# A delta-rule attention with a two-layer block behind it: unnormalised key triangles, keys ahead of queries, the first inverses apart, weights in eight pieces, an order table

## The chip, the core and the metric

The kernel runs on one core of a Trainium2 chip. The core has five engines that run side by side, each through its own instructions in order: TensorE (PE in the profile) multiplies matrices and writes to PSUM, VectorE (DVE), ScalarE (ACT) and GpSimd (POOL) work on tiles, and SyncE (SP) issues transfers. An instruction starts when the semaphores that it waits for have been raised; whatever stands behind it on its engine waits with it. The metric is the device time of one execution in microseconds (us). Before the change three runs gave a median of 319.31 us (317.59 to 320.36). The profile is of another execution, with a span of 320.9 us.

## The reference, cut to what matters

```python
k_n = k / (norm(k) + 1e-6)
for t in range(S):                       # S = 768 steps, for 4 batches x 8 heads, D = 48
    y[t]  = g[t] * (q[t] @ state)
    state = state + beta[t] * outer(k_n[t], v[t] - k_n[t] @ state)
x = y of all heads side by side          # 3072 tokens x 384
out = softplus(x @ w_in) @ w_out         # 384 -> 2048 -> 384
```

The recurrence over 768 steps is worked in chunks of 64 steps. In a chunk the update is a triangular system: with the Gram matrix of the chunk's keys, `T = (I + tril(beta K K^T))^-1 beta`, new values `U = T (V - K S)`, output `Q S + tril(Q K^T) U`, new state `S + K^T U`. The next chunk needs the state of the one before, so twelve chunks form a chain. The dense block behind it needs only the finished outputs of the chunks.

## The kernel before

**Tiling.** A tile holds one chunk of 64 steps of two batches on its 128 partitions (`r` picks the upper or lower 64), with a pair of batches `p` and the heads along the free side. A unit `u` is one head of one chunk; 16 units of chunk half `cl` of 0 and 1 make the 32 of a double chunk `cc` (128 steps, six of them). In a unit, rows are in quadrants of 32.

**Stages of a double chunk** (line numbers are those of the profile):

- *front*: the keys are squared on ScalarE (L380), summed on VectorE (L387), a root is taken (ScalarE L404 in the first double chunk, GpSimd `pow` L424 afterwards), 1e-6 is added (L433), inverted (L434), and the keys are scaled by it into float16 `kn` (L446); the queries are cast to `qn` (L467). For each `(cl, p)` TensorE transposes keys and queries together (L489), ScalarE copies all of it into `kqt` (L512), and 32 matmuls form the triangles of keys with keys and keys with queries (L531, L535). ScalarE copies the key part, negated, to `kk` (L553); VectorE masks the query part to `mt` (L572). So a key triangle waits for the norm and for the queries.
- *inverse*: VectorE turns `kk` so that each lane holds one unit (`ln`, L595); two multiplies by beta (L617) and 15 steps of a multiply and an add (L628, L635) invert the 16x16 diagonal blocks in `tt`, on VectorE for `cc` 0 and on GpSimd afterwards. VectorE turns the result back (L661, L683), ScalarE casts it (L671, L691), TensorE builds the 32x32 blocks (L710, L745, L755) and the coupling between them (L796, L799), with ScalarE copies between (L730, L779, L817). Both chunks of a double chunk share one inverse.
- *chain* of a chunk: keys times state (L843), `v` minus it (L886), inverse times it (L899), copy (L925), coupling (L954), copy (L981), state update (L997, L1020), output (L843 again, L1038), times `g` (L1071), transposed (L1088) into `xt` (L1098).
- *dense*: L1122 multiplies `xt` by `w_in` into PSUM `h`, ScalarE takes the softplus (L1143) into `ga`, L1160 multiplies by `w_out` into the one PSUM tile `o`, VectorE copies it out (L1182), SyncE stores it (L1191). The first and the last double chunk do this by single chunks, 256 tokens at a time, the others with 512.

**What sets the order.** Every piece of work is put down with an engine, a cost, its inputs, the buffers that it takes from rings and a priority. `Plan.run` plays the engines forward with these costs and writes the instructions of each engine in the order that comes out: of the ready pieces the one with the lowest priority number. It models transfers and the loading of TensorE's own instructions in blocks of 128 matmuls. On the chip that order is fixed; only the semaphores decide when each begins. Loads go out on SyncE (L299) in a written order: keys 0, queries 0, keys 1, values 0, gates 0, queries 1, values 1, keys 2, gates 1 (each number a double chunk). The two weights are one transfer each on GpSimd (L322, L335), which also turns them from float32 to float16; `w_in` is issued after values 0, `w_out` after queries 1.

Of the kernel before, what the change touches and what calls it, by code (L numbers as in the profile page):

```python
# [16 lines left out]

class Ring:


    def __init__(self, n, make):
        self.n, self.make = n, make
        self.live = 0
        self.freed = [0.0] * n
        self.count = 0


class Buf:
    def __init__(self, ring):
        self.ring = ring  # L30
        self.users = 0
        self.ap = None
        self.done = 0.0


class Item:
    __slots__ = (
        "eng", "cost", "fn", "deps", "bufs", "prio", "end", "tail", "n", "order", "mm", "dma",
# [3 lines left out]
class Plan:  # L42
    BLOCK = 128
    FETCH = 3.5

    def __init__(self):
        self.items = []

    def add(self, eng, cost, fn, deps=(), bufs=(), prio=0, tail=0.1, order=(), mm=0, dma=0):
        it = Item()  # L50
        it.eng, it.cost, it.fn = eng, cost, fn
        it.deps = [d for d in deps if d is not None]
        it.bufs, it.prio, it.tail, it.end = list(bufs), prio, tail, None
        it.n = len(self.items)
        it.order = [d for d in order if d is not None]
        it.mm, it.dma = mm, dma
        for b in it.bufs:
            b.users += 1
        self.items.append(it)
        return it  # L60

    def run(self):

        left = {}
        for it in self.items:
            left.setdefault(it.eng, []).append(it)
        free = {e: 0.0 for e in left}
        pipe = 0.0
        flight = []
        issued, arrive = 0, [0.0, 0.0]  # L70
        while any(left.values()):
            best = None
            for e, lst in left.items():
                cands = []
                for it in lst[:500]:
                    ready = 0.0
                    ok = all(d.end is not None for d in it.order)
                    for d in it.deps:
                        if d.end is None:
                            ok = False  # L80
                            break
                        t = d.end + (d.tail + 0.06 if d.eng != e else 0.0)
                        if t > ready:
                            ready = t
                    if not ok:
                        continue
                    need = {}
                    for b in it.bufs:
                        if b.ap is None:
                            need[b.ring] = need.get(b.ring, 0) + 1  # L90
                    for r, n in need.items():
                        if r.live + n > r.n:
                            ok = False
                            break
                        ready = max(ready, sorted(r.freed)[n - 1])
# [5 lines left out]
                can = [it for r, it in cands if r <= t0 + 1e-9]  # L101
                stall = 0.0
                if e == "PE":

                    def late(it):
                        last = (issued + it.mm - 1) // self.BLOCK
                        return max(0.0, arrive[min(last, len(arrive) - 1)] - t0 - it.cost)
# [3 lines left out]
                it = min(can, key=lambda x: (x.prio, x.n))  # L111
# [6 lines left out]
            for b in it.bufs:  # L118
                if b.ap is None:
                    r = b.ring  # L120
                    r.live += 1
                    r.freed.remove(min(r.freed))
                    b.ap = r.make(r.count)
                    r.count += 1
            it.fn()
            if it.dma:
                if e == "SP" and len(flight) >= 4:
                    t0 = max(t0, flight[-4])
                free[e] = t0 + it.cost
                pipe = max(pipe, free[e] + 0.6) + it.dma  # L130
                it.end = pipe + 1.4
                if e == "SP":
                    flight.append(it.end)
            else:
                it.end = free[e] = t0 + it.cost
            if e == "PE":
                block = issued // self.BLOCK
                issued += it.mm
                end = it.end
# [4 lines left out]
                it.end = free[e] = end  # L144
            for b in it.bufs:
                b.users -= 1
                b.done = max(b.done, it.end + it.tail)
                if b.users == 0:
                    b.ring.live -= 1
                    b.ring.freed.append(b.done)  # L150
        return max(free.values())
# [3 lines left out]
def kernel(  # L155
# [24 lines left out]
    consts = ctx.enter_context(tc.tile_pool(name="consts", bufs=1))  # L180
    pool = ctx.enter_context(tc.tile_pool(name="rings", bufs=1))
    psum = ctx.enter_context(
        tc.tile_pool(name="psum", bufs=1, space=bass.MemoryType.PSUM)
# [4 lines left out]
    def ring(name, n, shape, dt, where=pool):  # L188
        return Ring(n, lambda i: where.tile(shape, dt, tag=name, bufs=n, name=name))

    def fixed(name, n, shape, dt, init):
        tiles = [consts.tile(shape, dt, name=f"{name}{i}") for i in range(n)]
        for t in tiles:
            init(t)
        return Ring(n, lambda i: tiles[i % n])

    half_c = consts.tile([P, 32], F32, name="half_c")
    nc.vector.memset(half_c, 0.5)
    dummy = consts.tile([P, 1], F32, name="dummy")
    nc.scalar.activation(dummy, half_c[:, :1], AF.Sqrt)
    ident32 = consts.tile([P, P], F32, name="ident32")
    make_identity(nc, ident32)
    ident = consts.tile([P, P], F16, name="ident")
    nc.vector.tensor_copy(ident, ident32)
    beta_l = consts.tile([P, NSS, HC], F32, name="beta_l")

# [12 lines left out]
    mask = consts.tile([P, C], F16, name="mask")  # L223
# [11 lines left out]
    w_in = consts.tile([P, 3, FF], F16, name="w_in")  # L235
    w_out = consts.tile([P, NF, DM], F16, name="w_out")

    def pad0(t):
        nc.vector.memset(t[:, :, :, D:], 0.0)

    r_k = ring("kf", 4, [P, 2, H, D], F32)
    r_q = ring("qf", 3, [P, 2, H, D], F32)
# [3 lines left out]
    r_ss = ring("ss", 3, [P, 32], F32)  # L246
    r_kn = fixed("kn", 4, [P, 2, H, 64], F16, pad0)
    r_qn = fixed("qn", 2, [P, 2, H, 64], F16, pad0)

    r_kqt = ring("kqt", 10, [P, 2 * NP, 2 * C], F16)  # L250
    r_mt = ring("mt", 18, [P, NP, C], F16)
    r_kk = ring("kk", 2, [P, 2, U, HC], F16)
    r_ln = ring("ln", 1, [P, HC, HC], F16)
    r_n = ring("nn", 1, [P, 2, 16, 16], F32)

    r_t = fixed("tt", 1, [P, 2, 16, 48], F32, lambda t: nc.gpsimd.memset(t, 0.0))
    r_tmp = ring("tmp", 1, [P, 128], F32)
    r_t32 = ring("t32", 1, [P, HC, U], F32)
    r_tn = ring("tn", 2, [P, U, 16], F16)
    r_xs = ring("xs", 2, [P, U, 16], F16)  # L260
    r_td = ring("td", 2, [P, U, HC], F16)
    r_tn32 = ring("tn32", 1, [P, 16, U], F32)
    r_z = ring("z", 2, [P, U, HC], F16)
# [6 lines left out]
    r_o = ring("osb", 4, [P, DM], F32)  # L270
    p_d = ring("d", 5, [P, 512], F32, psum)
    p_h = ring("h", 2, [P, 512], F32, psum)
    p_o = ring("o", 1, [P, 512], F32, psum)

# [12 lines left out]


# [3 lines left out]
    def load(name, x, r, cc):  # L292
        for cl in range(2):
            b = Buf(r)
            t0 = cc * 128 + cl * C

            def fn(b=b, t0=t0, x=x):
                for b2 in range(2):
                    nc.sync.dma_start(  # L299
                        out=b.ap[64 * b2 : 64 * b2 + 64].rearrange(  # L300
# [925 lines left out]
```

## Time and profile before

| | |
|---|---|
| median of three runs | 319.31 us (317.59 to 320.36) |
| span of the profiled execution | 320.9 us |
| TensorE busy | 242.5 us (76%), 6384 matmuls |
| ScalarE, VectorE, GpSimd busy | 157.4, 134.9, 109.3 us |
| dense matmuls L1122 and L1160 | 77.0 and 73.6 us of TensorE's busy time |
| first L1122, first L1160 | at 74.2 and 84.9 us |
| loads of one chunk of one input | two transfers of 192 KB |
| `w_in`, `w_out`, issue to landing | 11.4 and 15.5 us |

The busy times overlap and are means over stages with different limits. The view of busy time by stretches shows where TensorE works, the lines of one engine in order of time show what its queue stood behind. A matmul's listed duration includes the pipeline; the distance between starts tells what the array can do. "issue" as releaser is time in which an engine waited for nothing that the profile shows.

### The profile page before, as it was taken

How to read it: one execution, taken by the hardware profiler on the slowest of the kernel's cores; microseconds unless marked ns; L12 is line 12 of the kernel's file. 1: busy time of each engine (PE TensorE's matmuls, PEld its weight loads, DVE VectorE, ACT ScalarE, POOL GpSimd, SP SyncE). 2: the span in 40 equal slices, each digit the busy share in tenths (PEclk: the TensorE clock that was granted, in tenths of full speed). 3: DMA queues.
4: the chain of work that ended last, by engine and by line, in shares of the span. 5: the costliest groups of instructions: out<-in, count | busy, mean ns of one | idle time of the engine just before them, and what ended most of it. 6: DMA issues, size and time to landing. Idle time of an engine off the chain costs nothing.

```text
span 320.9 us, 13899 instructions
## 1 busy us (share of the span) xinstructions
PE 242.5 (76%) x6384; PEld 160.9 (50%) x6384; DVE 134.9 (42%) x278; ACT 157.4 (49%) x272; POOL 109.3 (34%) x202
## 2 busy tenths in 40 slices
PE   0361081259769999988973969999799998998993
PEld 0240061247557775535653735566455565565761
DVE  2559635216452548573280548455053621321001
ACT  2381081534565654964463545745566247720630
POOL 8154133892015001889840061860008500000000
PEclk9999999999796999997985589999789999999999
DMA  8999999984980167921249390641100121012122
GB/s 117 165 163 182 181 170 192 158 121 86 154 157 8 29 121 137 167 53 27 53 85 144 61 144 3 102 89 41 29 2 4 30 51 29 4 25 51 25 50 51
DMA packets 106458, 27.73 MB, mean 86 GB/s; under 512 B 100768, under 2 KB 106016, under 8 KB 106400
## 3 DMA queue, kind: packets, MB, share of 16 engines
q1 hardware_dynamic: 103680, 23.60, 47.8%
q0 software_dynamic: 2720, 3.24, 6.0%
q8 instruction: 50, 0.82, 1.1%
q14 instruction: 8, 0.07, 0.1%
HBM read 25.26 MB, written 4.72 MB: 93 GB/s over the span
## 4 chain that ended last, share of the span: by engine, by line
PE 62%; DMA 8%; issue 8%; SPq 8%; ACT 5%; POOL 5%; DVE 4%; ACTq 0%; POOLq 0%
PE o L1160 19%; PE h L1122 19%; SPq L299 8%; DMA kf<-in_k_dram 4%; DMA qf<-in_q_dram 4%; PE d L489 3%; PE d L843 3%; PE d L1038 2%; PE d L954 2%; POOL tt L635 2%; PE d L899 2%; PE d L755 2%; POOL tmp L628 2%; PE d L799 2%; PE d L710 2%
## 5 line engine op out<-in xcount | busy, mean ns | idle before, releaser
L1143 ACT ACTIVATE ga<-h 128x512 f16<-128x512 f32 x96 | 57.0, 598 | 48.1 <-PE h L1122 46.2
L1122 PE MATMUL h<-xt,w_in 128*128 128x512 f16 (+1 forms) x384 | 77.0, 341 | 1.0 <-ACT ga L1143 0.9
L1160 PE MATMUL o<-w_out,ga 128*128 128x384 f16 x384 | 73.6, 333 | 2.8 <-DVE osb L1182 2.6
L1160 PEld LDWEIGHTS <-ga 128*128 128x128 f16 x384 | 36.5, 99 | 27.3 <-issue 5.8
L1122 PEld LDWEIGHTS <-w_in 128*128 128x128 f16 x384 | 35.4, 101 | 22.1 <-issue 3.4
L424 POOL TENSOR_TENSOR ss<-ss,half_c 128x32 f32<-128x32 f32 (+1 forms) x6 | 27.6, 4604 | 45.4 <-DVE ss L387 45.4
L1071 DVE TENSOR_TENSOR yg<-d,gf 128x384 f16<-128x384 f32 x24 | 13.2, 552 | 57.6 <-PE d L1038 49.1
L1182 DVE COPY osb<-o 128x384 f32<-128x384 f32 x24 | 13.3, 553 | 53.4 <-PE o L1160 53.3
L512 ACT COPY kqt<-d 128x1024 f16<-128x1024 f16 x24 | 23.7, 1012 | 23.2 <-PE d L489 23.2
L635 POOL TENSOR_TENSOR tt<-tt,tmp 128x30 f32<-128x30 f32 (+7 forms) x75 | 30.0, 400 | 5.9
L628 POOL TENSOR_TENSOR tmp<-nn,tt 128x30 f32<-128x30 f32 (+7 forms) x75 | 27.8, 370 | 5.9
L617 POOL TENSOR_TENSOR nn<-ln,beta_l 128x256 f32<-128x256 f16 x10 | 6.0, 618 | 54.6 <-DVE ln L595 54.6
L489 PE MATMUL d<-ident,qn 128*128 128x128 f16 x96 | 12.4, 269 | 15.9 <-POOL qn L467 14.7
L572 DVE TENSOR_TENSOR mt<-d,mask 128x256 f16<-128x256 f32 x48 | 18.1, 415 | 14.6 <-ACT kk L553 13.2
L553 ACT ACTIVATE kk<-d 128x256 f16<-128x256 f32 x48 | 16.3, 382 | 12.9 <-PE d L535 9.5
L489 PE MATMUL d<-ident,kn 128*128 128x128 f16 x96 | 12.4, 269 | 12.5 <-DVE kn L446 12.2
L387 DVE TENSOR_REDUCE ss<-ksq 128x16 f32<-128x768 f32 x12 | 11.3, 945 | 19.3 <-ACT ksq L380 19.3
L380 ACT ACTIVATE ksq<-kf 128x768 f32<-128x768 f32 x12 | 10.2, 848 | 16.1 <-DMA kf<-in_k_dram 14.6
L489 PEld LDWEIGHTS <-qn 128*128 128x128 f16 x96 | 8.8, 124 | 16.5 <-POOL qn L467 15.0
L531 PE MATMUL d<-kqt 48*64 48x128 f16 x384 | 13.4, 258 | 4.3 <-ACT kqt L512 2.9
L489 PEld LDWEIGHTS <-kn 128*128 128x128 f16 x96 | 8.3, 122 | 16.1 <-DVE kn L446 12.2
L981 ACT CAST u<-d 128x384 f16<-128x384 f32 x24 | 10.9, 482 | 10.7 <-PE d L954 10.5
(71 smaller groups left out, 325.8 us busy)
## 6 DMA issues: line engine op xcount, KB each, us to landing
kf<-in_k_dram SPq DMA_DIRECT2D x24, 192.0 KB, 5.8
qf<-in_q_dram SPq DMA_DIRECT2D x24, 192.0 KB, 5.6
vf<-in_v_dram SPq DMA_DIRECT2D x24, 192.0 KB, 5.2
gf<-in_g_dram SPq DMA_DIRECT2D x24, 192.0 KB, 5.3
out_dram<-osb SPq DMA_DIRECT2D x48, 96.0 KB, 2.6
w_in<-in_moe_w_in_dram POOLq DMA_DIRECT2D x1, 1536.0 KB, 11.4
w_out<-in_moe_w_out_dram POOLq DMA_DIRECT2D x1, 1536.0 KB, 15.5
beta_l<-in_beta_dram POOLq DMA_DIRECT2D x8, 12.0 KB, 4.3
```

Source lines behind the costliest of these rows:

```text
L299: nc.sync.dma_start(out=b.ap[64 * b2 : 64 * b2 + 64].rearrange("t p h d -> t (p h) d"), in_=x[2 * b2 : 2 * b2 + 2, :, t0 : t0 + C].rearran ...
L424: lambda ss=ss, r=r: nc.gpsimd.tensor_tensor(ss.ap[:, r], ss.ap[:, r], half_c[:, r], ALU.pow),
L489: nc.tensor.transpose(o[:, i, :, j], x.ap[:, p, 2 * i : 2 * i + 2].rearrange("p h d -> p (h d)"), ident,)
L512: lambda tp=tp, kq=kq: nc.scalar.copy(kq.ap.rearrange("p n c -> p (n c)"), f16ps(tp.ap)),
L531: nc.tensor.matmul(o[HALF[r], i], x[:, C:], x)
L553: nc.scalar.activation(kk.ap[:, :, u0 : u0 + 7 : 2].rearrange("p x i t -> p i x t"), g.ap.rearrange("p (i x t) -> p i x t", i=NP, x=4)[:, ...
L572: nc.vector.tensor_tensor(o.ap, g.ap.rearrange("p (i t) -> p i t", i=NP)[:, :, :C], mask[:, None, :].broadcast_to([P, NP, C]), ALU.mult,)
L628: eng.tensor_tensor(t, nn.ap[:, :, j + 1 :, j : j + 1].broadcast_to([P, 2, n, w]), tt.ap[:, :, j : j + 1, 16 : 16 + w].broadcast_to([P, 2, ...
L635: eng.tensor_tensor(rows, rows, t, ALU.add)
L1122: nc.tensor.matmul(hp.ap[:, n * b : n * b + n], w_in[:, j, f * P : (f + 1) * P], xt.ap[:, j, t0 : t0 + n], start=(j == 0), stop=(j == 2),)
L1143: lambda hp=hp, o=gb: nc.scalar.activation(o.ap, hp.ap, AF.Softplus),
L1160: nc.tensor.matmul(op.ap[:, :DM], b.ap[:, c + c0 : c + c0 + 128], w_out[:, f, :], start=(f == 0), stop=(f == NF - 1),)
```

## The change

It does the same mathematics in another order and places the work anew.

1. *Unnormalised keys.* `kn` is a plain cast of the keys. With the norm n of a key, the triangles come from the raw keys, and the inverse norms go where they are cheap: beta is divided by n squared in the layout of the inverse (`lane_beta`: a 32-wide transpose, a reciprocal, two small multiplies), and the values are multiplied by n (`vscale` on GpSimd, one multiply of a whole chunk; for the first chunk inside the existing VectorE operation). Front work no longer waits for the norm.
2. *Keys ahead of queries.* Keys and queries are transposed separately; the key triangle (64 matmuls per chunk) needs only the keys, the query triangle (32 matmuls) has its own PSUM tiles. Copies out of PSUM become fewer and wider for `kk` and `mt`, and are shared between ScalarE and VectorE.
3. *First inverses apart.* Chunk 0 gets an inverse of its own on VectorE, chunk 1 its own on GpSimd, the double chunks 1 to 5 one each on GpSimd. The root is taken on ScalarE for the first two double chunks.
4. *Weights and loads.* Each weight is loaded in four pieces, each issued when a given load has landed, and the dense matmuls wait for their piece alone. Loads go by chunk: keys 0, keys 1, values 0, queries 0, gates 0, keys 2, keys 3, queries 1, values 1, gates 1, then keys two chunks ahead.
5. *Planner and order table.* The planner now counts switches of TensorE's tiling, gives buffers in order, and models transfers differently; engine and priority of every piece come from a table of 1164 words (a letter for the engine, a number for the priority). Rings change: `kf` 4 to 3, `qf` 3 to 2, `qn` 2 to 3, `tt`, `nn`, `tmp`, `ln` 1 to 2, `td`, `z` 2 to 3, `osb` 4 to 3.

The chain of a chunk and the dense block keep their matmuls.

```diff
-            sc_en, sc_eng = ("POOL", nc.gpsimd) if cc == 1 else ("DVE", nc.vector)
-            def scale(kf=kf, o=kn[cl], ss=ss, cl=cl, eng=sc_eng):
-                eng.tensor_tensor(o.ap[:, :, :, :D], kf.ap, ss..., ALU.mult)
+    def cast(c, name, ring_, prio, en):
+        alt = {"DVE": 0.57, "POOL": 0.83, "ACT": 0.83}
+            lambda en, f=f, o=o: copy(en, o.ap[:, :, :, :D], f.ap),
...
+    def lane_beta(cc, nv, nv_it, prio):
+            nc.vector.transpose(nl.ap, nv.ap)
+            nc.vector.reciprocal(nl.ap, nl.ap)
+            nc.vector.tensor_tensor(bl.ap, beta_l[:, cc], nl.ap, ALU.mult)
+            nc.vector.tensor_tensor(bl.ap, bl.ap, nl.ap, ALU.mult)
...
+            for p, en in enumerate(("ACT", "DVE")):
+                ev.append(add(en, "kev", 0.6 if p == 0 else 0.4, fn, deps=[t1], ...))
+            if j == 1:
+                t2 = add("PE", "gramk", 0.75, gram, deps=ev, ...)
+            else:
+                t2 = add("PE", "gramq", 0.45, gram, deps=its[0] + its[1], ...)
...
+            def vscale():
+                nc.gpsimd.tensor_tensor(vf.ap, vf.ap, nv..., ALU.mult)
...
+    for c in range(2):
+        kk_it = front(c, kk, -400 + 20 * c, 12, "DVE", "POOL", ("ACT", "DVE"))
+        nv_it, _ = norms([c], nv, -405 + 20 * c, True)
+        inverse([c], kk, kk_it, bl, bl_it, c == 0, False, -450 + 60 * c, -430 + 60 * c)
...
+    weights(0, (("v", 0), ("q", 0), ("k", 2), ("k", 3)))
+    weights(1, (("q", 1), ("v", 1), ("g", 1), ("g", 1)))
...
+    plan.use(_TABLE)
     plan.run()
```

## The prediction

> **What bounds the kernel now.** I read the forty slices first, to find where TensorE idles.
>
> ```profile
> PE   0361081259769999988973969999799998998993
> PEclk9999999999796999997985589999789999999999
> DMA  8999999984980167921249390641100121012122
> ```
>
> A slice is 8 us. Over the first nine TensorE does little and the transfers are full; from the tenth on it is the engine that is busy, with a hole in slices 21 to 23. The busy time by stretches puts numbers on it:
>
> ```profile
> 0.00:20.00 20.00, 5.00 (x65) 4.02 (x66) 8.35 (x21) 7.94 (x12) 9.56 (x21) 1.00 1.23 145
> 20.00:40.00 20.00, 3.70 (x102) 2.51 (x102) 15.19 (x46) 4.94 (x11) 7.50 (x6) 1.00 1.23 178
> 40.00:60.00 20.00, 8.00 (x284) 6.34 (x282) 7.87 (x13) 10.29 (x16) 9.55 (x20) 1.00 1.31 175
> ...
> 160.00:180.00 20.00, 12.53 (x587) 9.99 (x586) 10.68 (x20) 8.86 (x13) 4.26 (x12) 0.67 0.62 97
> ```
>
> After span comes TensorE's busy time: 16.7 us of the first 60. Full transfers suggest a kernel that waits for data. The queues in order of time say what it really waits for. VectorE:
>
> ```profile
> 37.47 0.19 DVE L635 TENSOR_TENSOR tt<-tt,tmp 128x30 f32<-128x30 f32 x1
> 42.89 0.75 DVE L572 TENSOR_TENSOR mt<-d,mask 128x256 f16<-128x256 f32 x2 [5.23 <-ACT kk L553]
> ...
> 50.23 0.99 DVE L661 STREAM_TRANSPOSE tn<-tt 128x512 f32<-128x512 f32 x1
> ```
>
> The first inverse is done at 37.7 us, and the transpose that carries it on starts at 50.2, because the masks of the next double chunk stand ahead of it. They wait for queries:
>
> ```profile
> 38.88 0.82 POOL L467 CAST qn<-qf 128x768 f16<-128x768 f32 x1 [9.70 <-DMA qf<-in_q_dram]
> ```
>
> ScalarE repeats the fault with keys that aren't needed yet:
>
> ```profile
> 57.28 0.84 ACT L380 ACTIVATE ksq<-kf 128x768 f32<-128x768 f32 x1 [4.94 <-DMA kf<-in_k_dram]
> 58.03 1.93 ACT L691 CAST td<-t 128x1024 f16<-128x1024 f32 x1
> ```
>
> So 20.4 us (37.7 to 58.0) pass in two queues blocked at their heads, and the first L1122 comes at 74.2. The hole at 160 has a like cause: GpSimd, which owns the inverses, waits 26.5 us for the `ln` of the third double chunk and starts it at 127.2, so the dense work of the first two runs out before the third's chain is done.
>
> ```profile
> POOL nn L617 <- DVE ln L595: 54.6, 3, 26.5
> ```
>
> The slow clock there is a consequence. At full rate four transposes start within 0.23 us (114.16 to 114.40); at 180.16 they take 0.40 and at 15.2 0.43.
>
> **What the skill says.** "TensorE: Matmul & The Clock Gate", Part 1, has the array at half rate until it has been busy for some 3.4 us and again after a gap of that order. The transposes just named agree (0.23 against 0.43), though the printed clock is 1.00 in the first 80 us. "Runtime: NRT & Kernel Launch", Instruction fetch mechanics, has instructions arriving in blocks of 16 KiB, 256 each. The trace has 50 such transfers (0.82 MB) for 12,768 TensorE instructions, and 26 us of "issue" on the chain that ended last; the skill calls this mostly hidden, which the trace contradicts in bursts of small matmuls (3.3 us before 172.2). "DMA: Bandwidth & Descriptors", Queues, rings and completion order, has all queues sharing the same 16 engines. Four query issues took 11.4 us beside `w_in`, against 4.7 undisturbed.
>
> **The parts.** *A start that needs one chunk of keys.* The first keys have landed at 6.0 (first L380). Cast 0.56 (VectorE's L467 row); eight cold transposes 0.86; two copies of 512 at about 0.6 in parallel; 64 triangles about 1.6 (16 + 16 at L531 and L535 take 0.91 cold); the negated copy 0.6 (as L817, 591 ns): 10.2. `ln` 1.9, with a reduce of 0.95 perhaps ahead: 13.0. Two multiplies 0.8; fifteen steps 8.9 (28.8 to 37.7): 22.7. Two transposes back 2.3, and half of the 1.94 us cast: 26.0. From the first L745 to the first L1122 the trace has 14.2 us (60.0 to 74.2), 4.3 of it "issue": 9.9 without. First L1122 near **36** (34 to 42), 38 us sooner. The norm (square 0.85, reduce 0.95, root 0.2, then five small VectorE operations, about 1.1 together with reference to L433 and L434) is hidden behind the triangles.
>
> *Are data and weights there?* A chunk of one input takes 2.35 us (half of 4.7), a weight adds some 7 (11.4 and 12.2 against 4.7). Seven inputs and `w_in`: 2 + 16.5 + 7 = 25.5. Three more and `w_out`: 39.5, all; the first L1160 came 10.7 us after the first L1122, so pieces arriving between 31 and 40 are in time, and a dense matmul that waits for its piece alone can start before the rest. Four pieces instead of one cost GpSimd issue time, 0.6 each against 0.84 and 1.25 for the wholes: at most 3 us in the gaps before its first inverse. But a piece waits for a load's landing, and behind it on GpSimd stand query casts and chunk 1's inverse; who waits for that is chunk 1's chain, not chunk 0's.
>
> *The triangles* go from 64 to 96 matmuls a chunk with less width: at full rate 1.16 us a chunk before (0.58 per 32); between 1.16 and 1.75 (three times 0.58) after. I take 1.2, as the wide halves vanish. 384 matmuls more are three more instruction blocks, noise. *Copies:* ScalarE loses `kqt` 23.7 and `kk` 16.3 for 14 + 7, VectorE gains about 17 for these and loses the key scaling (9.5) and most casts (5.4); both are far below TensorE, so nothing on the path. *GpSimd* per double chunk: four casts at 0.83, two `vscale` at 1.48 (its L446 row), a `pow` 5.44, an inverse 15.1 (0.53 + 0.24 + 1.2 at L607, L608 and L617, then 13.1 for the fifteen steps from 54.6 to 67.7): **26.8** us. TensorE needs 34.6 (below), so it is hidden if it starts early. `vscale` is also a new wait in the chain: the subtraction at L886 now needs it, on an engine whose queue may hold an inverse. Ordered behind one it would hold the whole chain, and the next chunk with it, for up to 15.1 us; ordered a chunk ahead it costs nothing, since values land early (the trace has a single wait for values, 8.5 us, put down to a load at the start). I take nothing, and 15 us at the worst, which the range has to hold. Two `tt` buffers remove the wait of L607 on L683 (18.8 us). Fewer `kf` and `qf` can make loads start later; the loads and stores take 11.8 us a chunk against 17.3 of TensorE.
>
> *TensorE's own work*, from full-rate start-to-start distances between 100 and 160 us: transposes 0.90, triangles 1.16, L710 0.56, L755 0.65, L799 0.43, L843 twice 0.74, L899 0.61, L954 0.50, L997 0.32, L1038 0.62, L1088 0.34: 6.8 a chunk; dense 5.25 + 5.2: 10.5. Together 17.3, times 12: **207 us**. Before, some 15 of it was done by 74.2, so 192 took 246.7 us: 55 over. By stretches, from idle time and clock: 74 to 100 lost 9, 160 to 190 about 18, 190 to 232 6, the end (one `o` tile, copies and last store) 7, the rest the remainder.
>
> *Sum.* 36 to the first L1122. 10 us of array work is done by then (chunk 0 6.8, chunk 1's front 2, a bit of chunk 2), 197 left. Losses I expect: the start's contention 9, as before; the hole of 18 + 6 shrinks to 8, since the third inverse can begin near 60 and no longer at 127; the end 7; the rest, 15 before, I put at 9, between half and all of it, because the planner now counts what a switch of tiling costs. 36 + 197 + 33 + 4 for the last copy and store = **270 us**.
>
> **Rivals.** *The start alone* is gained, the later holes stay: 36 + 197 + 51 + 4 = **288**. For it: an order fixed ahead by costs has already failed twice in this trace. Against it: the hole came from late inverses, which this change brings forward. *GpSimd's queue as the bound*: it takes on casts, `vscale`, a sixth inverse and eight issues; if in-order waiting keeps it from running ahead, each double chunk costs 26.8 + 5 (front) + 20 (two chains of 10) = 52, and 47 + 5 x 52 + 21 + 4 = **332**, slower. For it: L617 and L424 waited 100 us in all here. Against it: those waits were idle time of GpSimd, not its work, and the norm and queries that blocked it are out of the way. *Gain at the start given back*: the dense work catches up with the chain and waits for transfers and inverses, ending near **318**. Against it: loads are worth 11.8 of 17.3 us a chunk. *Nearly full overlap*: losses 15 in all, **252**.
>
> **Chances.** 270: 0.57. 288: 0.24. 252: 0.08. 318: 0.03. 332: 0.08. The range 250 to 298 takes in the first two with the bounds of the first L1122 (34 to 42), of the triangles (up to 7 us) and of the losses (15 to 55). Faster by over 1%: 0.88; within: 0.03; slower: 0.09.
>
> **What would show it.** First L1122 at 34 to 42, and VectorE's transpose of the first inverse directly behind the last step. TensorE above 80% busy from 40 us on, clock above 0.95 in its middle. GpSimd starts the third double chunk's inverse before 75 and its sum stays below 170 us. It is wrong if GpSimd or an "issue" row leads TensorE's waits, if transposes at 0.4 us per four are seen after 100 us, or if L1160 waits for `w_out`.

## The result and the profile after

The changed kernel takes **307.78 us** (median of four, 305.89 to 309.16) beside 319.84 for the kernel before on the same chip: a ratio of 0.9598, 95% interval [0.9519, 0.9678]. It is 4% faster; the prediction was 270 us, 16%, with a range that ended at 298. (Ratios here leave disturbed runs out, which is why a median sometimes lies higher than its ratio suggests.)

The slices of the profiled execution (span 307.5 us, so 7.7 us each), to be laid beside those of before:

```profile
PE   0130183277988997899987999959999899999993
PEclk9999999999999999969997999987999979999999
DMA  8999439999015979699298430843000111021122
```

The hole in the middle is closed, and from the eleventh slice on (77 us) TensorE is above 80% busy, as forecast, but for slices 16, 22, 27 and the last. What did not come is the early start: slices 2 to 9 are as empty as before. There is also something new, a dip of the transfers in slices 5 and 6 with a full stretch behind it. The same in stretches of 20 us:

```profile
0.00:20.00 20.00, 3.31 (x112) 2.31 (x112) 6.02 (x24) 6.22 (x11) 13.69 (x27) 1.00 1.22 149
20.00:40.00 20.00, 2.10 (x104) 1.68 (x104) 18.94 (x40) 2.91 (x5) 10.93 (x26) 1.00 0.78 113
40.00:60.00 20.00, 10.62 (x519) 8.56 (x519) 15.52 (x26) 11.11 (x21) 16.02 (x33) 1.00 1.03 152
...
160.00:180.00 20.00, 17.86 (x591) 11.30 (x589) 9.77 (x18) 12.08 (x22) 9.03 (x5) 0.91 0.72 121
```

From 0 to 60 us TensorE is busy for 16.0 us, against 16.7 before; from 160 to 180 for 17.9 against 12.5. The waits of GpSimd say why the middle is better. The row that had 54.6 us now has

```profile
POOL nn L612 <- DVE ln L591: 13.6, 3, 10.3
```

and the third double chunk's inverse begins at 97.7 instead of 127.2. The first dense matmul, in the lines of TensorE in order of time:

```profile
72.11 0.36 PE L786 MATMUL d<-s,kqt 48*64 48x48 f16 x11 [1.99 <-issue]
72.39 0.50 PE L877 MATMUL d<-u,z 32*32 32x48 f16 x16
72.83 1.46 PE L1014 MATMUL h<-xt,w_in 128*128 128x256 f16 x6
```

It starts at 72.8, against 74.2 before and 36 in the prediction (L1014 is the L1122 of before, L1044 its L1160). From there to the end 234.7 us pass; the prediction had 234.

*Where the start went.* GpSimd in order of time:

```profile
6.75 3.55 POOL L272 MEMSET kk<- 128x2048 f16 x2
10.24 0.24 POOL L275 MEMSET nv<- 128x32 f32 x3
10.42 2.69 POOL L272 MEMSET tt<- 128x1536 f32 x2
13.17 0.82 POOL L314 CAST kn<-kf 128x768 f16<-128x768 f32 x1
```

The cast that starts everything stands behind 6.4 us of memsets. In the kernel before they were 1.4 us for one `tt`; here there are two `tt` and two `kk`. The keys had landed at 6.1; the first transposes (L485) run at 14.05. VectorE at the end of the first inverse:

```profile
37.06 0.19 DVE L629 TENSOR_TENSOR tt<-tt,tmp 128x30 f32<-128x30 f32 x1
37.29 1.03 DVE L647 STREAM_TRANSPOSE tn<-tt 128x512 f32<-128x512 f32 x1
38.25 1.26 DVE L663 STREAM_TRANSPOSE t<-tt 128x512 f32<-128x512 f32 x2
```

The transpose is directly behind the last step, as forecast; before it stood 12.5 us behind. But the fifteen steps took from 24.4 to 37.25, 12.8 us instead of 8.9. GpSimd works on chunk 1's steps at the same time until 35.6 us and then waits; from there on VectorE is as fast as before (0.24 us for a 128x78 operation, against 0.33 beside GpSimd). The waits of TensorE up to the first L1014 (us in total, times, longest):

```profile
PE d L485 <- POOL kn L314: 28.3, 2, 14.2
PE d L711 <- issue: 4.3, 1, 4.3
PE d L684 <- ACT tn L654: 3.2, 1, 3.2
PE d L684 <- issue: 3.1, 1, 3.1
PE d L786 <- issue: 2.0, 1, 2.0
PE d L527 <- issue: 1.6, 1, 1.6
```

The "issue" rows have a pattern. If the matmuls are counted from the start, the stalls come at numbers 479, 607, 735, 863 and 991, exactly 128 apart, with 1.8, 3.2, 4.4, 1.7 and 2.2 us from start to start: 13.3 us in all. The first four as the trace lists them, with the idle time before each in brackets:

```profile
48.69 0.23 PE L527 MATMUL d<-kqt 48*32 48x64 f16 x1 [1.60 <-issue]
55.16 0.45 PE L684 MATMUL d<-tn,kk 16*32 16x16 f16 x38 [3.08 <-issue]
61.63 0.33 PE L711 MATMUL d<-td,xs 32*16 32x16 f16 x27 [4.26 <-issue]
66.73 0.71 PE L485 MATMUL d<-ident,kn 128*128 128x128 f16 x5 [1.35 <-issue]
```

In the same time the trace has transfers of 16 KiB on the instruction queue at 46.2, 52.8, 59.4, 63.9 and 69.3, and TensorE goes on 2.2 to 2.8 us after each has begun. So 128 matmuls, each with its weight load, are a block, and a block comes when it comes. The first L1014 is number 1018 in TensorE's order (882 in the kernel before). The small matmuls themselves need little of the array: L684 and L711 take 8 to 10 ns each from start to start, 1.3 us for 128. The planner counts on 3.5 us for a block (`FETCH`). The pattern goes on behind the first L1014: over the whole execution, TensorE stands for more than 0.5 us ahead of 18 such matmuls, 30.5 us in all.

### The profile page after: what moved, and what is told of

The parts are those of the page before. It is cut to its first block, busy times and chain, and to the rows that moved or that the text cites. A ratio compares the mean times of both kernels' runs of the same rounds, so it can differ in the third digit from the quotient of the medians.

```text
span 307.5 us, 14779 instructions
## 1 busy us (share of the span) xinstructions
PE 236.3 (77%) x6768; PEld 155.8 (51%) x6768; DVE 158.9 (52%) x306; ACT 142.9 (46%) x240; POOL 142.6 (46%) x262
## 4 chain that ended last, share of the span: by engine, by line
PE 61%; DVE 12%; issue 11%; POOL 11%; ACT 4%; POOLq 0%; ACTq 0%
PE h L1014 19%; PE o L1044 18%; PE d L485 3%; POOL tt L629 3%; POOL tmp L622 3%; PE d L684 2%; PE d L786 2%; DVE tt L629 2%; PE d L840 2%; PE d L939 2%; DVE tmp L622 2%; PE d L711 2%; DVE ln L591 2%; PE d L561 2%; PE d L877 2%
## 5 line engine op out<-in xcount | busy, mean ns | idle before, releaser
L1044 PE MATMUL o<-w_out,ga 128*128 128x384 f16 x384 | 77.9, 343 | 3.2 <-issue 1.9
L1014 PE MATMUL h<-xt,w_in 128*128 128x512 f16 (+1 forms) x384 | 74.8, 336 | 1.0 <-issue 1.0
L1044 PEld LDWEIGHTS <-ga 128*128 128x128 f16 x384 | 35.7, 101 | 26.1 <-issue 7.3
L1014 PEld LDWEIGHTS <-w_in 128*128 128x128 f16 x384 | 36.1, 100 | 21.7 <-issue 3.4
L485 PE MATMUL d<-ident,kn 128*128 128x128 f16 x96 | 9.7, 258 | 30.8 <-POOL kn L314 28.3
L312 ACT ACTIVATE kqt<-d 128x512 f16<-128x512 f16 x26 | 15.0, 596 | 26.2 <-PE d L485 24.5
L314 DVE CAST u<-d 128x384 f16<-128x384 f32 x25 | 13.4, 552 | 26.3 <-PE d L877 18.5
L443 POOL TENSOR_TENSOR nv<-nv,half_c 128x32 f32<-128x32 f32 x4 | 22.0, 5509 | 7.4 <-DVE nv L423 7.4
L485 PEld LDWEIGHTS <-kn 128*128 128x128 f16 x96 | 7.1, 115 | 32.8 <-POOL kn L314 28.7
L571 DVE TENSOR_TENSOR mt<-d,mask 128x512 f16<-128x512 f32 x24 | 15.7, 683 | 9.9 <-PE d L561 9.8
L808 POOL TENSOR_TENSOR vf<-vf,nv 128x768 f32<-128x768 f32 x11 | 16.2, 1476 | 8.2 <-DMA vf<-in_v_dram 5.0
L961 DVE TENSOR_TENSOR yg<-d,gf 128x384 f16<-128x384 f32 x24 | 12.8, 551 | 10.1 <-PE d L939 10.0
L314 DVE COPY kqt<-d 128x512 f16<-128x512 f16 x22 | 9.1, 422 | 14.6 <-ACT kqt L312 9.0
L423 DVE TENSOR_REDUCE nv<-ksq 128x16 f32<-128x768 f32 x12 | 11.4, 949 | 9.6 <-POOL nv L275 7.8
L312 ACT ACTIVATE u<-d 128x384 f16<-128x384 f32 x23 | 10.7, 490 | 10.7 <-PE d L840 7.4
L829 DVE TENSOR_TENSOR w<-vf,d 128x384 f16<-128x384 f32 x22 | 11.3, 547 | 8.2 <-PE d L786 4.5
L591 DVE STREAM_TRANSPOSE ln<-kk 128x1024 f16<-128x1024 f16 x7 | 13.3, 1905 | 4.2 <-ACT kk L312 4.0
```

The source lines that it names most:

```text
L312: nc.scalar.activation(o, x, AF.Copy, scale=float(sign))
L314: ENG[en].tensor_copy(o, x)
L443: lambda: nc.gpsimd.tensor_tensor(nv.ap[:, sl], nv.ap[:, sl], half_c[:, sl], ALU.pow),
L485: nc.tensor.transpose(o[:, NP * p + i], x.ap[:, p, 2 * i : 2 * i + 2].rearrange("p h d -> p (h d)"), ident,)
L571: nc.vector.tensor_tensor(o.ap, gm[m].ap.rearrange("p (n t) -> p n t", n=H), mask[:, None, :].broadcast_to([P, H, C]), ALU.mult,)
L591: lambda: nc.vector.transpose(ln.ap, kk.ap[:, 1].rearrange("p u t -> p t u")),
```

## The experiments

All but the first have the order of the changed kernel written out, so that each edit stands alone; an edit of the order is shown as the pieces that move. "First L1014" and the time at which the transposes L979 of chunks 2 and 3 are done are read from the profiled executions, one of each kernel. The sets ran on different chips, each with the kernel before beside it. The changed kernel itself gave a ratio of 0.9598 in one set and of 0.9710 in another, so a difference of about 1% between kernels of different sets says nothing.

The expectations call competing explanations "theories" and give them letters. In the first ones F is the stream of TensorE's instructions and Q the work of the other engines; in the text for both first inverses on VectorE, F is the chain of chunk 0 and Q the instruction blocks.

**The table alone.** The plan is made without the table, with the engines and priorities in the code.

```diff
-    plan.use(_TABLE)
     plan.run()
```

> The changed kernel without its order table: engines and priorities are those written beside each piece. Key casts for chunks 0 and 1 are then on VectorE, chunk 0 goes first. Theories Q and F both expect an earlier first L1014, near 50 to 58 us. If the table is what costs the gain, the total is below 300; if the table's worth lies in the middle (fewer holes after 80 us) and theory B holds, 305 to 320.

Ratio to before 0.9864 [0.9801, 0.9927]; the median, 321.01 us, is just above the 305 to 320 expected. First L1014 at 53, twenty us earlier than with the table, and still slower. From 80 to 160 us its TensorE is busy for 60.7 us, with the table for 72.6, although its granted clock there is the lower one (0.87 against 0.96). So half to two thirds of the gain (1.5 to 2.7%, by the two ratios of the changed kernel) are the table's and lie in the middle; the rest of the change alone brings some 1.4%, by the medians 0.6% (321.01 beside 322.98).

**The memsets.**

```diff
     def pool0(t):
-        nc.gpsimd.memset(t, 0.0)
+        nc.vector.memset(t, 0.0)
```

> The order of every engine is that of the changed kernel; only the clearing of kk and tt at the start moves from GpSimd to VectorE, so that the first key cast, which the order table put on GpSimd, no longer stands behind 6.2 us of memsets (it began at 13.2 us, with keys landed at 6.1). Theory Q (the first L1014 is late because VectorE, ScalarE and GpSimd hold chunk 0's work back): everything up to the first L1014 shifts by 5 to 7 us, L1014 from 72.8 to 66 or 67. Theory F (it is late because 1018 matmuls stand ahead of it in TensorE's stream and instructions arrive at 5 to 6.5 us per 128 matmuls): the stream is consumed from 128 to 479 earlier, so the first stalls come earlier too, but the loads that fill the DMA engines don't; 68 to 71. Theory B (the later holes set the end): total within 1% of 307.8 in either case.

302.66 us, 0.9379 [0.9298, 0.9459]. First transposes at 8, first L1014 at 66.7, as theory Q said, chunks 2 and 3 at 113, the median 5 us lower. Everything up to there shifts by 5 to 6 us, and the end with it: this cost was on the path, theory B on the total fails, and this kernel is faster than both others.

**Chunk 0 first.** What chunk 0 needs, and the keys of chunk 1, go ahead of the rest; TensorE has 484 matmuls before the first L1014.

```diff
-tr k0, gram k0, tr k1, gram k1, tr k2, L684 c0, tr k3, ..., all of chain 0 and half of chain 1, L1014 c0
+tr k0, gram k0, tr k1, gram k1, L684 c0, ..., chain 0, L1014 c0 (two groups), then the rest as it was
```

> The changed kernel with the order of the first part rewritten: chunk 0's own work and the key half of chunk 1's front go first on every engine, then the first two L1014 groups; all else follows in the order that it had. The first L1014 then stands behind 484 matmuls and not 1018. Theory F: the first four blocks of instructions are loaded before they are needed, so the first L1014 comes about 13 us after the inverse, at 52 to 56 us. Theory Q: TensorE's place in the stream is not what holds it; VectorE and ScalarE still do the same pieces ahead of it, so 65 to 70. Total: if the start is worth its time, 290 to 296; theory B: 303 to 308, because chunk 1's chain and the later inverses come no sooner.

314.17 us, 0.9713 [0.9640, 0.9786]. First L1014 at 52, as theory F said, and the kernel is no faster than the changed one (0.9598 and 0.9710); both totals expected were lower. The waits of TensorE from 14 to 80 us begin with

```profile
PE d L684 <- ACT tn L654: 20.8, 2, 18.1
```

The 18.1 us of it end at 38.65: they are the wait for chunk 0's own inverse, ahead of all dense work. Behind the first L1014 TensorE waits only 2.7 us for chunk 1's inverse, though that comes ten us later than in the changed kernel (the cast L670 that carries it on begins at 59.6 instead of 49.6). From 60 to 80 us TensorE is busy for 10.3 us, against 14.3 in the changed kernel, and chunks 2 and 3 are done at 123 instead of 118.

**Dense work early.** The same order with all dense work of chunk 0 directly behind its first two groups; then the same with the memsets moved. The "hole of 18 us" of the first expectation is the wait just named, which dense work can't fill, since it needs chunk 0's inverse itself.

```diff
+... L1014 c0 (two groups), L1014 and L1044 c0 (all), then the rest as it was
```

> The order with chunk 0 ahead, and all sixteen groups of its dense work (L1014, L1044) ahead of what is left of chunk 1, so that they fill the hole of 18 us. Theory B (what counts is array work that is ready early): the hole shrinks to under 8 us and the time is 300 to 305 us instead of 314. Rival: what is put ahead pushes chunk 1's chain back by as much, chunk 2's transposes L979 stay at 123 or come later, and the time is 311 to 317 us.

> The order of the previous kernel with the GpSimd memsets on VectorE. Theory B: the 5 to 6 us that the memsets cost add up with the fill: 295 to 300 us. Rival (block supply takes over): no more than 2 us under the same order without the edit.

327.23 us, 1.0048 [1.0001, 1.0095], and 319.68 us, 0.9861 [0.9805, 0.9917]. In the first the rival wins, and by more than it claimed: chunks 2 and 3 are done at 135 instead of 118. In the second (132) neither expectation holds: the level is far from 295 to 300 us, but moving the memsets brings 1.9%, some 6 us, as theory B had it, and not 2 us at most. There the first L1014 runs at 43.2, and then this (waits of TensorE, 43 to 110 us):

```profile
PE h L1014 <- DMA w_in<-in_moe_w_in_dram: 9.0, 1, 9.0
PE d L711 <- issue: 6.8, 3, 4.1
```

The dense work stands at the head of TensorE's queue, waits for its weights, and holds chunk 1 back: its first L684 runs at 73.5 instead of 51.8. An early first L1014, by itself, is worth nothing: at 43 the ratio is 0.9861, at 52 it is 1.0048 or 0.9713, at 73 it is 0.9598 or 0.9710. What the end goes with is chunk 3. Thirteen kernels, the changed one and its repetition among them, keep the table's order in the later chunks and have the same number of matmuls or two whole blocks more. In all of them the execution ends 185.4 to 190.8 us after the transposes of chunk 3, which are done between 111.8 and 135.5 us.

**Both first inverses on VectorE.**

```diff
-        inverse([c], kk, kk_it, bl, bl_it, c == 0, False, -450 + 60 * c, -430 + 60 * c)
+        inverse([c], kk, kk_it, bl, bl_it, True, False, -450 + 60 * c, -430 + 60 * c)
```

> Undoes one part: chunk 1's first inverse runs on VectorE behind chunk 0's instead of beside it on GpSimd. Theory C (the two engines slow each other down): chunk 0's fifteen steps take 8.5 to 9.5 us instead of 12.8, chunk 1's end near 46, as before the edit, although they now wait for their turn. On the time: theory F (the chain of chunk 0 sets the first L1014) expects it 3 to 4 us earlier, near 69, and 302 to 305 us; theory Q (the instruction blocks set it, L1014 being matmul 1018) expects it within 1.5 us of 72.8 and 306 to 309 us.

313.19 us, 0.9625 [0.9563, 0.9687]. The group of the adds on VectorE, first in the changed kernel, then here (durations min/median/max):

```profile
L629 DVE TENSOR_TENSOR tt<-tt,tmp x15: 191/449/774, 24.6 to 37.1; 128x30 f32<-128x30 f32 x2, 128x56 f32<-128x56 f32 x2, 128x78 f32<-128x78 f32 x2, 128x96 f32<-128x96 f32 x2
```

```profile
L629 DVE TENSOR_TENSOR tt<-tt,tmp x30: 190/265/2306, 24.7 to 47.8; 128x30 f32<-128x30 f32 x4, 128x56 f32<-128x56 f32 x4, 128x78 f32<-128x78 f32 x4, 128x96 f32<-128x96 f32 x4
```

Theory C holds: chunk 0's steps take 8.6 us with GpSimd quiet. Both theories on the time fail, since the first L1014 comes at 77: key casts and copies on VectorE now stand behind chunk 1's steps. So the slowdown costs chunk 0 some 4 us, and giving it up gains nothing: the ratio lies between the two of the changed kernel.

**More matmuls at the start.** L684 of chunk 0 is done five times.

```diff
-                for u in range(16 * cl, 16 * cl + 16):
+                for u in list(range(16 * cl, 16 * cl + 16)) * (5 if cs[0] == 0 else 1):
```

> The changed kernel with the 64 matmuls of L684 for chunk 0 written five times over (same result), which puts 256 matmuls, two blocks of instructions, ahead of the first L1014. They are small: at the 10 ns apiece of the row before they are worth 2.6 us. Theory F: two more blocks at 5 to 6.5 us each, the first L1014 at 83 to 86 us. Theory Q: 75 to 76.

First L1014 at 78.7, 5.8 us later for 256 matmuls that need the array for 2.6 us, and between the two expectations. The time, 316.79 us, is a single run on another chip, and gives no measure of what two blocks cost in all.

**The loads.** Three query buffers again, which let SyncE go on; then the later weight pieces ahead of chunk 1's inverse; then both with the memsets moved; then the pieces in the middle of that inverse, with the clear L599 moved behind it.

```diff
-    r_q = ring("qf", 2, [P, 2, H, D], F32)
+    r_q = ring("qf", 3, [P, 2, H, D], F32)
```

```diff
-GpSimd: steps of chunk 1 (..., w_out, step, w_out, w_in, vscale, w_out, w_out, ..., w_in), inverse of double chunk 1
+GpSimd: w_in, w_in, w_out x4, steps of chunk 1, inverse of double chunk 1
```

> Same order; the ring of query tiles has three buffers again, as in the kernel before (the room is taken from one buffer each of the cast queries and of w16, of which the order never holds more than one and two). Theory W (the 11 us in which SyncE waits for a query buffer push the loads into 48 to 75 us, where they slow the instruction blocks down): the blocks between 40 and 75 us come less than 5 us apart on average instead of 5.6, the first L1014 is at 67 to 70, and the time 302 to 305 us. Rival: the loads fill whatever time there is, blocks stay 5.6 apart, first L1014 at 72 to 74, 306 to 309 us.

> Same order but for GpSimd's six later weight pieces, which are issued right after chunk 0's gate has landed, ahead of chunk 1's inverse, instead of at 43 to 52 us behind its steps. In the changed kernel the transfers stand still from 34 to 44 us and then take over 1.2 of the engines' time until 64 us, where the instruction blocks come 6.6 us apart, against 3.7 to 5 where the share is under 0.9. Theory W (loads slow the blocks, and the blocks set the first L1014): the share from 46 to 62 us falls under 1.0, the blocks there come at most 5.5 apart, first L1014 at 68 to 70.5, 303 to 306 us. Rival (spacing has another cause, or the chain of buffers takes over): first L1014 at 72 to 74, 306.5 to 309 us.

> The previous kernel with the GpSimd memsets on VectorE. Theory W: both gains add, first L1014 at 62 to 65, 297 to 300 us. Rival: no better than the memsets alone, first L1014 at 66 to 67.5, 301.5 to 304 us.

> The previous kernel with three query buffers too. If the loads that wait for a query buffer still matter once the weights are out of their way, first L1014 comes 1 to 3 us earlier than in the previous kernel; otherwise within 1 us of it. From the rule that the end comes 189 us after the second pair's transposes L979 in all orders derived from the changed kernel, the time is that of these transposes plus 188 to 191 us in all three kernels.

> The kernel with the GpSimd memsets on VectorE (302.7 us), with the six later weight pieces moved up into the time in which its transfers stand still (32 to 38 us) and its GpSimd waits 4 us for VectorE's L663 to free the buffer that L599 clears for the third double chunk; that clear moves behind chunk 1's last step. Unlike the kernel with the pieces at the very start, the keys of chunks 2 and 3 keep their place ahead of them. Theory W: share of the transfers from 40 to 56 us under 1.1 instead of 1.28, blocks at most 5.5 us apart instead of 6.5 to 7.3, first L1014 at 62 to 65, chunk 2's transposes L979 at 108 to 111, 298 to 301 us. Rival (what the loads gain is lost to chunk 1's values and gates, which come later): first L1014 at 66 to 68, 302 to 304 us.

The new dip of the transfers is a wait for a query buffer, in SyncE's lines of the changed kernel:

```profile
28.77 2.23 SPq L344 DMA_DIRECT2D kf<-in_k_dram  x2
42.12 1.31 SPq L344 DMA_DIRECT2D qf<-in_q_dram  x2
```

The third buffer closes the dip (the share of the transfers from 34 to 44 us rises from 0.04 to 1.04), but the stretch behind it is as full as before (1.29 from 46 to 62 us), and the first L1014 stays at 72.5: its rival holds. The median is that of the changed kernel (307.38 us), the ratio lower (0.9471 [0.9425, 0.9517]); whether it gains a per cent stays open. The early pieces do what theory W says of the blocks. The stretch from 46 to 62 us in the changed kernel, then with the pieces early (the last but one column is the share of the transfers: the time of all packets over that of the 16 engines, which can pass 1):

```profile
46.00:62.00 16.00, 5.56 (x356) 4.54 (x357) 9.84 (x14) 5.46 (x10) 10.59 (x21) 1.00 1.29 188
```

```profile
46.00:62.00 16.00, 7.94 (x456) 6.55 (x455) 10.55 (x17) 6.35 (x12) 7.17 (x16) 1.00 0.90 143
```

With the share down from 1.29 to 0.90 the blocks that begin in this stretch come 4.6 us apart instead of 6.6, a hundred more matmuls run, and the first L1014 is at 68.7. But the gains don't add: 307.24 us (0.9452 [0.9292, 0.9612], too wide to tell), 303.07 with the memsets (0.9432 [0.9347, 0.9517]), 303.68 with the buffer too (0.9442 [0.9347, 0.9536]), 302.83 with the pieces in the middle (first L1014 at 65.6 where 62 to 65 was expected; two of its six runs took 296 and 300 us, the others 303 to 304, too uneven for a ratio). None is shown to be better than the memsets alone. In the kernel with memsets and early pieces, TensorE waits 4.0 us for the cast of chunk 3's keys, and that 4.3 us for their load, which the weights have pushed back; with the pieces in the middle, the stalls move forward with the loads (4.5 us at matmul 479). What the blocks gain in one place the loads take back in another.

**Number of matmuls or array time?** In chunks 0 to 3, most products of L711 and L877 are left out; in another kernel their array time is given back in 40 large matmuls ahead of L705; in a third only these are added. The changed kernel runs beside them.

```diff
-                for u in range(16 * cl, 16 * cl + 16):
+                for u in range(16 * cl + (15 if cs[0] < 4 else 0), 16 * cl + 16):
...
-            for pi in range(H):
+            for pi in range(H - 1 if c < 4 else 0, H):
```

```diff
+                for _ in range(10 if cs[0] < 4 else 0):
+                    nc.tensor.matmul(uv(ep.ap)[:, us], ident, ident[:, None, :].broadcast_to([P, 2, P]))
```

> Leaves out part of the computation: in chunks 0 to 3, sixty of the 64 products of L711 (the correction of the lower inverse) and 28 of the 32 of L877 per chunk, 352 small matmuls in all, which the profile of the changed kernel gives 240 x 10 ns + 112 x 20 ns = 4.7 us of array time. Every wait and copy stays. Supply theory (blocks of 128, 4.5 us apart, set the pace up to 118 us): 352/128 x 4.5 = 12 us earlier, chunk 2's transposes at 106 to 109, 294 to 298 us. Array theory: 4.7 us earlier, 113 to 115, 302 to 304 us.

> The same 352 small matmuls left out, and ten 128x256 matmuls put in front of L705 in each of chunks 0 to 3, 40 x 119 ns = 4.8 us (L1014 takes 0.467 ns for a column), so that the array has the same work in 312 fewer matmuls. Supply theory: 312/128 x 4.5 = 11 us earlier, 296 to 300 us. Array theory: as the changed kernel, 306 to 309 us.

> Only the forty 128x256 matmuls added, nothing left out: 4.8 us more array time in 40 matmuls. Supply theory: 40/128 x 4.5 = 1.4 us later, 308 to 310 us. Array theory: 4.8 us later, 311.5 to 314 us.

> The changed kernel itself, its plan written out, on the same chip: 306 to 309 us by either theory; it is the measure for the three runs beside it.

| chunks 0 to 3 | matmuls | array time | median us | ratio to before | chunk 3 done at | from there to the end |
|---|---|---|---|---|---|---|
| changed kernel | 6768 | as it is | 310.74 | 0.9710 [0.9639, 0.9780] | 121.6 | 190.8 |
| large ones added | +40 | +4.8 us | 311.19 | 0.9622 [0.9522, 0.9721] | 127.1 | 184.7 |
| small ones left out | -352 | -4.7 us | 298.61 | 0.9275 [0.9197, 0.9353] | 116.6 | 182.8 |
| left out, large ones added | -312 | as it is | 299.06 | 0.9316 [0.9260, 0.9371] | 118.2 | 179.8 |

In total, array time is not what costs: the two kernels with fewer matmuls agree within 0.5 us, and within their intervals, although 4.8 us of array work lie between them, and both are 12 us under the changed kernel. That is the 11 to 12 us that 4.5 us for each block of 128 gave. (The changed kernel itself came out 2 us above the 306 to 309 expected of it.)

In place, neither theory holds. Chunk 3 is done 5.5 us later, 5.0 earlier and 3.4 earlier, where the supply theory had 1.4 later, 12 and 11 earlier, and the array theory 4.8 later, 4.7 earlier and no change. (With the large ones added, the granted clock from 40 to 80 us was 0.66 in this execution, against 1.00 in the others.) Behind chunk 3 the same 4384 matmuls are left in all four kernels, and the three edited ones need 6 to 11 us less for them. All three lie below the 185.4 to 190.8 us of the thirteen kernels named above. An average of 4.5 us between blocks doesn't settle it either: it is first of all the time over the number of matmuls. What the three kernels have in common is that 40, 352 or 312 matmuls shift the place at which each block ends among the later matmuls; no run tests whether that is the cause. So the same cut was made in chunks 4 to 7:

> Leaves out the same 352 small matmuls of L711 and L877, but in chunks 4 to 7, and gives their array time back in forty 128x256 matmuls. If the number of matmuls sets the pace all along: 0.93 of the kernel before, as with the cut in chunks 0 to 3, some 299 us beside 322. If it does so only in the start, and the array afterwards: no change from the changed kernel, 0.96 to 0.975, 308 to 312 us beside 322.

> Leaves out the 352 small matmuls in chunks 4 to 7 and gives nothing back. If the array sets the pace there: 4.8 us under the previous kernel; if the number of matmuls does: within 1 us of the previous kernel, both near 299 us.

301.84 us, 0.9430 [0.9359, 0.9501], with the array time given back; 303.39 us, 0.9445 [0.9366, 0.9524], without. Again no difference between the two, so array time isn't what counts there either. The gain over the changed kernel is 1.5 to 2.8% by its two ratios, 5 to 9 us, where 0.93 was expected if the number counts all along. From chunk 3 to the end these kernels need 179.8 and 180.8 us, which would fit the number of matmuls, had not the same stretch become as short with nothing left out in it.

The stalls of the blocks tell a part of it. Ahead of every 128th matmul, TensorE stands for 29.7 us in all in the repeated changed kernel (stalls above 0.5 us) and for 21.1 us with 312 matmuls fewer in chunks 0 to 3; 7.3 of the 8.6 us between them lie before 120 us. How the later gain is made up stays open: from chunk 3's transposes to the end, the busy time of TensorE falls from 173.6 to 165.2 us, at a granted clock of 0.97 against 0.86 in the first 50 us of it, but runs of the same kernel at 0.94 over the whole span were as fast.

## Why the prediction was wrong

The direction was right, the size was not. By its own steps:

- *"First L1122 near 36 (34 to 42)"* failed; it is 72.8. The missing 36.8 us, term by term:

  | stretch | prediction | measured | what stood between |
  |---|---|---|---|
  | keys landed to first transposes | 0.6 | 8.0 | zero fills ahead of the key cast |
  | to the first step of the inverse | 7.2 | 10.4 | `ln` of both chunks (1.88 each) ahead of chunk 0's steps |
  | the fifteen steps | 8.9 | 12.8 | GpSimd's own inverse beside VectorE's |
  | inverse to `td` | 3.3 | 3.4 | |
  | `td` to the first L1122 or L1014 | 9.9 | 32.2 | the order of TensorE, and the blocks |

  The zero fill of `kk` is new and that of `tt` doubled, which the prediction passed over, and it put the cast on VectorE with nothing ahead of it; the table puts it on GpSimd. That GpSimd slows VectorE down is shown by the kernel with both inverses on VectorE. The Trainium skill, "SBUF — State Buffer", SBUF: two separate sides, says that a VectorE operation with two SBUF inputs and a GpSimd operation that reads SBUF share a port pair, one waiting for the other; the steps are such operations on both sides, and the trace agrees for VectorE (0.27 to 0.45 us), while GpSimd loses little (0.39 and 0.40 us at the median, against 0.36 and 0.39 in later double chunks). The last term is the largest, 22.3 us too small. The prediction took the path of one chunk, with "issue" taken off. In the table's order the whole chain of chunk 0, half of chunk 1's and fronts of chunks 2 to 4 stand before it, 866 matmuls from L684's first, and 13.3 us of the time are visible stalls for blocks. With chunk 0 ahead of the rest this stretch took 11.9 us, so some 20 of the 22 us are the order's, the stalls in it included; with the memsets moved as well, the first L1014 came at 43.2.
- *The sum behind it.* The 234 us from there to the end were 234.7. That is in part luck: the sum took 10 us of array work as done by then, but more matmuls stood ahead of the first dense one than before (1018 against 882, to which the prediction gave some 15 us), so less work was left and more was lost. And the step that adds an early start to a fixed rest is wrong: the kernel with L1014 at 43.2 needs 277 us from there. TensorE works in order, so dense work put early waits for weights and holds the next chunk's inverse back. That is the rival "gain at the start given back", to which the prediction gave 0.03 and 318 us; the kernel that does start early takes 319.7.
- *"384 matmuls more are three more instruction blocks, noise"* failed as a step: a count of the same size, 352 matmuls, or 312 with the array time the same, was worth 12 us in one set and 5 to 9 in another. Put down to the number alone, the 12 us would be some 4.8 us a block and 14 us for the 384, an estimate from that one set; since most of the gain came where nothing had been left out, the price of a block is not shown. The stalls are. The small matmuls of L711 occupy the array for 10 ns each, 128 of them for 1.3 us, and their blocks came 4.5 us apart and more. The prediction, after the Trainium skill's "Runtime: NRT & Kernel Launch", Instruction fetch mechanics, had blocks of 256 instructions, which is 128 matmuls with their weight loads and fits the stalls; it saw the contradiction to "mostly hidden" and left it out of the sum. Summing start-to-start distances "at full rate" counts the array in stretches in which a block is already there.
- *The hole*: "18 + 6 shrinks to 8" held in the main. The stretch from 160 to 180 us gained 5.3 us of TensorE time, though the third inverse began at 97.7, not before 75. GpSimd's sum is 142.6 us, under the 170 named, and its queue is not the bound: the rival of 332 us is refuted, as is the nearly full overlap of 252. The new wait for `vscale`, which the sum took as nothing, was small: VectorE's L829 waited 2.5 us for GpSimd in all.
- *"TensorE above 80% from 40 us on"* holds only from 77 us on, but for three slices and the last. Of the signs of error that the prediction named, two came true: GpSimd leads TensorE's waits (28.3 us for the cast of keys, both times in the start), and "issue" leads them between 46 and 73 us. Transposes after 100 us start within 0.18 us per four but for two neighbouring fours at 133 us (about 0.3), and L1044 does not wait for `w_out`.
- *Weights*: "pieces arriving between 31 and 40 are in time" failed for the later ones: GpSimd issued them between 43 and 52 us, behind chunk 1's steps. No dense matmul waited for them here, as the first L1014 was later still, but their loads filled the stretch from 46 to 62 us: issued early, they brought the first L1014 from 72.8 to 68.7.

Shown are the memsets (5 us or more), the slowdown between VectorE and GpSimd (4 us of the chain), the order as the cause of the late first L1014, the table's worth in the middle (1.5 to 2.7%), the uselessness of an early L1014 by itself, and that fewer small matmuls shorten the kernel by more than their array time. Not shown is by which path they do so, nor how much of the time up to chunk 3 would go with faster blocks: nothing here speeds the supply without moving loads.

## What to carry over

Count TensorE's instructions as well as its array time: where small matmuls prevail, look in the trace for stalls at every 128th, and compare the spacing of the blocks with the array's time for the same stretch. When an experiment gives the total that a theory forecast, look whether the gain lies where the theory put it. Before a start is called early, look at what stands ahead of it in each engine's order, memsets of new buffers included, and ask what the next stage will have ready; a first result that comes sooner than its successors only moves the hole.

## What the runs showed of the hardware

- VectorE's additions of the inverse (float32, 128x30 to 128x128) took 0.45 us at the median while GpSimd ran the same kind of operation, 0.27 us with GpSimd quiet; GpSimd's took 0.39 and 0.40 us beside them, 0.36 and 0.39 us later on.
- Blocks of TensorE's instructions came 6.5 to 7.3 us apart where the loads took over 1.2 of the engines' time, 4.4 to 4.7 us at a share of 0.9, and never less than 3.3 us apart. After a stall TensorE went on 2.2 to 3.2 us after the transfer of its block began, though the transfer itself took 0.9 to 1.5 us.
- Forty 128x256 matmuls (4.8 us of array time) made no difference clear of noise to a kernel whose array the page calls 77% busy, though 352 small ones left out brought 12 us: a busy share of TensorE near 90% (173.6 of the 190.8 us behind chunk 3) doesn't mean that array time is what is short.
